# Experts 1 to 7 in float32 from whole-expert weight places, in an attention and two-FFN kernel

## The chip, the cores and the metric

The kernel runs on one core of a Trainium2 chip. The metric is the time of one execution on the device in microseconds: the median over runs, 895.2 us for the kernel before (three runs, 892.25 to 896.22). The profile is of one execution of its own.

## The reference, cut to what matters

Three steps follow one another. Block-causal attention over 4 batches, 8 heads, 576 positions and 64 columns gives 2304 tokens of 512 columns. A leaky FFN follows, whose weights are float64. The last step is a mixture of experts:

```python
do_compute = x @ w_skip > 0                    # the others pass through
logits = x @ w_gate;  e_idx = argmax(logits)   # one of 8 experts for a token
h = np.maximum(x[mask] @ w1[e], 0.0)           # 512 -> 1024
y[mask] = gate_w * (h @ w2[e])                 # 1024 -> 512
out = x + y
```

Each expert has 2 MB of w1 and 2 MB of w2 in float32. How many tokens an expert has is known only when the kernel runs.

## The kernel before, in words

Phase A is the attention with the first quarter of the FFN, phase B the rest of the FFN over six blocks of 384 tokens (`b_mm1`, `b_mm2`), each followed by its routing. What this document is about comes last, the experts.

**Precision.** Most products are made from three float32r matmuls: each operand is split into a high part, rounded to float32r, and a low part, the remainder, and high x high, high x low and low x high are summed in PSUM (`products`, L852). The attention's first four pairs of heads (`WHOLE`, L23) instead multiply in float32 at one point, the product with V (L285).

**One expert tile** (`expert_tile`, L885) takes 128 gathered tokens. `turn_x` (L844) transposes them on PE; ACT copies the high part, DVE subtracts the low part. `m1` has two halves of 12 matmuls of 512 columns; ACT applies relu (L897), PE transposes the hidden layer (`turn_h`, L902), ACT copies its high part (L903), DVE subtracts its low part (L904), and `m2` has 24 matmuls of 512 columns. `finish` scales the sum and adds the residual on DVE (L941) and scatters the rows to the output from POOL (L942). The matmuls are held in the program's order (`keep_in_program_order`); other instructions are put in order by a planner, which issues what is ready.

**The weights.** A piece is 128 rows of 512 columns. `load_piece` (L795) loads it from SP's queue to one of twelve places (tiles "raw", "cv2", "cv3"); `split_piece` (L815) casts it to its high part on ACT or DVE (L825), subtracts the low part on DVE or POOL (L826), and then issues the load that takes its place. An expert has 16 pieces, and each has its parts in one of two buffers (`w1buf`, `w2buf`), which lie in the FFN's weight tiles `wbt[0..5]` and in its input `xT`. While one expert multiplies, its tile's `fill` splits the next expert's 16 pieces, in portions (`SOME`, `SOME1`). Loads of expert 1 beyond the first six pieces are `held` back behind the loads of the lists, in program order (L1012).

**Which tiles run.** Expert 0 has up to four tiles and a loop, experts 1 to 7 one tile, then conditional ones. Each condition is a `tc.If` on the expert's count (L1043), so each engine takes a branch there; expert 7 as a whole stands in such a condition (L1030). The scatters show eleven tiles in this run: four of expert 0, one each of experts 1 to 6, and a second one of expert 2. Expert 7 has no tokens, and its pieces are split all the same, during expert 6. A tile's `ahead` transposes the tokens of the next tile before its own last matmuls.

**Order before the experts.** Expert 0's first tile runs beside the routing of the last block. Its second tile's tokens come by a gather that POOL issues behind that routing, then POOL writes the lists, and SP loads them back (`load_lists`, L599) once the first tile has ended; four more gathers follow.

Of the kernel before, what the change touches and what calls it, by code (L numbers as in the profile page):

```python
# [347 lines left out]
def attention_moe_kernel(  # L348
# [27 lines left out]
    NB = NT // BT  # L376
    HALF = NT // 2
    KS = 4

    SOME, SOME1 = (3, 4, 3, 6), (0, 2, 4, 10)  # L380

    C = ctx.enter_context(tc.tile_pool(name="c", bufs=1))
    DR = ctx.enter_context(tc.tile_pool(name="dr", bufs=1, space=DRAM))
# [392 lines left out]
    def lane(L, n, xg, xt):  # L776

        return dict(li=L["li"][:, n], ix=L["ix"][:, n], xg=xg, xh=xt[0], xl=xt[1],
                    xT=[(xt[0][:, c], xt[1][:, c]) for c in range(ND)])


    pair = lambda x, y: [[wbt[(x, y)[c // 2]][:, i, c % 2 * F2 : c % 2 * F2 + F2] for c in range(ND)] for i in range(2)]
    w1buf = [pair(wi_at[0], wi_at[1]), pair(wi_at[2], wo_at[2])]
    w2buf = [[[xT[i][:, f % ND, f // ND * D : (f // ND + 1) * D] for f in range(NF2)] for i in range(2)],
             [[wbt[wo_at[f // 4]][:, i, f % 4 * D : f % 4 * D + D] for f in range(NF2)] for i in range(2)]]


    tags = ("raw", None, "cv2", "cv3") * 3
# [1 line left out]

    begin = [NP - NF2 + f for f in range(ND)] + list(range(NP - NF2)) + [NP - NF2 + f for f in range(ND, NF2)]
    AHEAD = len(tags)
    raws, held = {}, []

    def load_piece(i):  # L795
        e, j = divmod(i, NP)
        j = j if e else begin[j]
        if e >= E:
            return
        nm = tags[i % AHEAD]  # L800
        n = 2 if nm == "raw" else 1
        t = CV.tile([128, n, 512], F32, name=nm, bufs=3)
        for k_ in range(n):
            raws[i + k_] = t[:, k_]
        if j < NP - NF2:
            h, c = divmod(j, ND)
            src = w1[e, c * 128 : (c + n) * 128, h * 512 : h * 512 + 512]
        else:
            f = j - (NP - NF2)
            src = w2[e, f * 128 : (f + n) * 128, :]  # L810
        ld = nc.sync.dma_start(t, src.rearrange("(n p) w -> p n w", p=128))
        if i in held:
            tc.keep_in_program_order(ld)

    def split_piece(i):  # L815
        e, j = divmod(i, NP)
        j = j if e else begin[j]
        a, b = w1buf[e % 2], w2buf[e % 2]
        if j < NP - NF2:
            h, c = divmod(j, ND)  # L820
            hi, lo = (a[k_][c][:, h * 512 : h * 512 + 512] for k_ in range(2))
        else:
            hi, lo = (b[k_][j - (NP - NF2)] for k_ in range(2))
        r = raws.pop(i)
        tc.keep_in_program_order(nc.vector.tensor_copy(hi, r) if i % 4 == 3 else nc.scalar.copy(hi, r))  # L825
        (nc.gpsimd if i % 3 == 2 else nc.vector).tensor_tensor(out=lo, in0=r, in1=hi.bitcast(F32), op=ALU.subtract)  # L826
        nm = tags[i % AHEAD]
        if nm == "raw":
            return
        nxt = i + AHEAD - (nm is None)  # L830
        if e == 0 and nxt >= NP + 6:
            held.append(nxt)
        else:
            load_piece(nxt)

    upto = [0]

    def w_steps(n):

        l = [lambda i=i: split_piece(i) for i in range(upto[0], min(n, E * NP))]  # L840
        upto[0] = max(n, upto[0])
        return l

    def turn_x(lx, pt=None, pinned=True):  # L844
        pin = tc.keep_in_program_order if pinned else lambda ins: ins
        pt = ps3.tile([128, ND, 128], F32, name="pt", tag="ps") if pt is None else pt
        for c in range(ND):
            pin(nc.tensor.transpose(pt[:, c], lx["xg"][:, c * 128 : (c + 1) * 128], ident))
        nc.scalar.copy(lx["xh"], pt)
        nc.vector.tensor_tensor(out=lx["xl"], in0=pt, in1=lx["xh"].bitcast(F32), op=ALU.subtract)  # L850

# [30 lines left out]
                    pt=lambda: bank("acc1", 4, 128),  # L882
                    yo=lambda: CV.tile([128, 512], F32, name="cv2", bufs=3))

    def expert_tile(e, lx, fill=(), ahead=(), late=False, at=None, between=None):  # L885

        a, b = w1buf[e % 2], w2buf[e % 2]
        at = at or places()
        hh, hl, ph, py = at["hh"], at["hl"], at["ph"], at["py"]
        fs = [slice(f * 512, f * 512 + 512) for f in range(2)]  # L890
        m1 = [products(ph[f], lx["xT"], [(a[0][c][:, fs[f]], a[1][c][:, fs[f]]) for c in range(ND)]) for f in range(2)]
        m2 = products(py, [(hh[:, c], hl[:, c]) for c in range(NF2)], [(b[0][c], b[1][c]) for c in range(NF2)])
        h = {}

        def relu(f):
            h[f] = at["hs"](f)
            nc.scalar.activation(out=h[f], in_=ph[f], func=AF.Relu)  # L897

        def turn_h(f):
# [6 lines left out]
        fill, share = list(fill), SOME1 if late else SOME  # L906

        def some(n):
            run_all(fill[:n])
            del fill[:n]  # L910

        some(share[0])
# [6 lines left out]
        some(share[1])  # L919
        relu(0)  # L920
        run_all(m1[1][:7])
        if between:
            between[2]()
        turn_h(0)
        some(share[2])
        run_all(m1[1][7:])
        relu(1)
        if not late:
            run_all(ahead)
        run_all(m2[:4])  # L930
        turn_h(1)
        some(share[3])
        run_all(m2[4:18])
        if late:
            run_all(ahead)
        run_all(m2[18:])
        some(len(fill))
# [8 lines left out]
        return finish  # L946

    seq = [(n, f) for a, b in cuts for n in order[:3] for f in range(a, b)]
    seq += [(n, f) for n in order[3:] for f in range(NFB)]
# [45 lines left out]
    finish = expert_tile(0, first, at=places_early(),  # L995
                         ahead=[lambda: turn_x(second, ps2.tile([128, ND, 128], F32, name="rtx", tag="acc0", bufs=1), True)], late=True,
                         between=(lambda: run_all(begin_r), lambda: run_all(route_r), place_and_put))
    end = finish()
    cnti = RC.tile([128, E], I32, name="cnti")
# [8 lines left out]
    with tc.issue_after(end.ins):  # L1008
        for k_ in (2, 1, 0, 3):
            load_lists(lall[k_], lambda l: l.rearrange("(e n) c -> n e c", e=E)[k_ * 128 : (k_ + 1) * 128], nc.sync)  # L1010
            find(lall[k_])
    for i in held:  # L1012
        load_piece(i)
    p2.close()
    ps3 = ctx.enter_context(tc.tile_pool(name="ps3", bufs=7, space=PSUM))
    M3 = ctx.enter_context(tc.tile_pool(name="m3", bufs=2))
# [4 lines left out]
    firsts = [lane(lall[0], e, xgs[e % 4], xts[e % 2]) for e in range(E)]  # L1021
    fourth = lane(lall[3], 0, xgs[0], xts[2])
    for lx in (firsts[1], fourth, firsts[2], firsts[3]):
        gather(lx)
    for e in range(E):
        ahead1 = [lambda: turn_x(firsts[e + 1])] if e + 1 < E else []
        some = ExitStack()
        if e:
            if e == E - 1:
                some.enter_context(tc.If(nreg[e] > 0))  # L1030
            second = lane(lall[1], e, xgs[4], xts[2])
            gather(second)
            finish = expert_tile(e, firsts[e], w_steps((e + 2) * NP), ahead1, at=places(True))

        def later(k_):
            if e == 0 and k_ == 3:
                return fourth
            L, n = (lall[k_], e) if k_ < KS else (llate, 0)
            return lane(L, n, xgs[4 + (k_ + 1) % 2], xts[2 + (k_ + 1) % 2])

        def more(k_, lx):
            filled = e == 0 and k_ == 1
            with nullcontext() if filled else tc.If(nreg[e] > 128 * k_):  # L1043
                if k_ == 1 and not filled:
                    turn_x(lx)
                if k_ < KS:
                    ahead = []
                    nx = later(k_ + 1)
                    if k_ + 1 < KS:
                        if nx is not fourth:  # L1050
                            gather(nx)
                        ahead = [lambda: turn_x(nx)]
                    finish = expert_tile(e, lx, w_steps(2 * NP) if filled else (), ahead + (ahead1 if filled else []), True)
                    finish()
                    more(k_ + 1, nx)
                else:
                    with tc.For_i(KS, (nreg[e] + 127) // 128, 1) as i:
                        load_lists(llate, lambda l: l[bass.ds(i * 128 + e * NT, 128), :].unsqueeze(1), nc.sync)
                        find(llate)
                        gather(lx)  # L1060
                        turn_x(lx)
                        expert_tile(e, lx)()

        more(1, second)
        if e:
            finish()
        if e + 4 < E:
            gather(firsts[e + 4])
        some.close()
# [31 lines left out]
```

## Time and profile before

| | |
|---|---|
| median of three runs | 895.2 us |
| profiled execution, its span | 892.16 us, 890.3 us |
| PE busy | 804.6 us, 90% |
| DVE, ACT, POOL busy | 532.4, 463.3, 401.9 us |
| mean granted clock of TensorE | 0.98 |
| moved by DMA | 110.64 MB, 124 GB/s over the span |

The span runs from the first to the last instruction. Matmuls are pipelined and overlap in the records, so a pace is read from start to start. "PEq", "DVEq" and the like are the engines' sequencers, which handle branches and waits. The last stretch, some 200 us, is the experts'.

### The profile page before, as it was taken

How to read it: one execution, taken by the hardware profiler on the slowest of the kernel's cores; microseconds unless marked ns; L12 is line 12 of the kernel's file. 1: busy time of each engine (PE TensorE's matmuls, PEld its weight loads, DVE VectorE, ACT ScalarE, POOL GpSimd, SP SyncE). 2: the span in 40 equal slices, each digit the busy share in tenths (PEclk: the TensorE clock that was granted, in tenths of full speed). 3: DMA queues.
4: the chain of work that ended last, by engine and by line, in shares of the span. 5: the costliest groups of instructions: out<-in, count | busy, mean ns of one | idle time of the engine just before them, and what ended most of it. 6: DMA issues, size and time to landing. Idle time of an engine off the chain costs nothing. (4 is left out here: it accounts for less than half of the span.)

```text
span 890.3 us, 13976 instructions
## 1 busy us (share of the span) xinstructions
PE 804.6 (90%) x4754; PEld 717.1 (81%) x4754; DVE 532.4 (60%) x1026; ACT 463.3 (52%) x1054; POOL 401.9 (45%) x472
## 2 busy tenths in 40 slices
PE   6789999999999988989999999999999869788683
PEld 4567899989989987879989898989899658566462
DVE  6887888878787896894132222121133671776897
ACT  5787779878787866662222222222234232534453
POOL 3766446455455664653324333222243350544463
PEclk9999999999999999999999999999999989999998
DMA  6664563563431255732204150302022691664772
GB/s 163 154 168 120 158 149 91 128 186 89 104 85 43 76 175 142 250 129 77 71 1 115 64 153 25 107 1 70 26 60 98 146 318 52 211 228 159 245 248 86
DMA packets 120596, 110.64 MB, mean 124 GB/s; under 512 B 77285, under 2 KB 87525, under 8 KB 120496
## 3 DMA queue, kind: packets, MB, share of 16 engines
q1 hardware_dynamic: 112320, 93.35, 36.3%
q0 software_dynamic: 8176, 16.06, 6.1%
q8 instruction: 51, 0.84, 0.4%
q14 instruction: 49, 0.40, 0.1%
HBM read 78.87 MB, written 22.68 MB: 114 GB/s over the span
## 5 line engine op out<-in xcount | busy, mean ns | idle before, releaser
L441 PE MATMUL ph<-xT,wbt 128*128 128x384 f32 x864 | 164.9, 339 | 4.3 <-ACT cv L488 2.5
L441 PE MATMUL acc<-gh,wbt 128*128 128x384 f32 x576 | 162.1, 341 | 3.6 <-DVE x2T L773 2.5
L441 PEld LDWEIGHTS ph<-xT,wbt 128*128 128x128 f32 x864 | 152.2, 189 | 4.9 <-ACT cv L488 2.7
L433 POOL TENSOR_TENSOR gl<-u,gh 128x384 fp32r<-128x384 f32 x72 | 74.6, 1036 | 177.4 <-ACT gh L432 177.3
L432 DVE TENSOR_TENSOR u<-ph,u 128x384 f32<-128x384 f32 x72 | 40.0, 555 | 179.3 <-ACT u L431 179.3
L441 PEld LDWEIGHTS acc<-gh,wbt 128*128 128x128 f32 x576 | 105.1, 188 | 11.3 <-issue 8.0
L185 POOL TENSOR_SCALAR P<-P,stat 128x128 f32<-128x128 f32 (+2 forms) x144 | 78.6, 567 | 58.2 <-DVE stat L183 43.9
L441 PE MATMUL acc<-gl,wbt 128*128 128x384 f32 x288 | 97.8, 340 | 0.6 <-POOL gl L433 0.6
L432 ACT CAST gh<-u 128x384 fp32r<-128x384 f32 x72 | 36.9, 512 | 93.2 <-PE acc L441 90.3
L431 ACT ACTIVATE u<-ph 128x384 f32<-128x384 f32 x72 | 35.3, 490 | 93.7 <-PE ph L441 88.2
L285 PE MATMUL pv<-ph,vs 128*128 128x320 f32 (+4 forms) x280 | 70.0, 319 | 2.1 <-DVE ph L239 0.8
L236 PE MATMUL pt<-ident,P 128*128 128x128 f32 x400 | 63.5, 286 | 3.8 <-ACT P L174 2.7
L161 PE MATMUL sp<-wbt 128*128 128x128 f32 (+2 forms) x192 | 55.5, 371 | 10.8 <-DMA wbt<-wbt 3.3
L441 PE MATMUL po<-gA,woa 128*128 128x320 f32 (+1 forms) x384 | 60.2, 302 | 3.4 <-DVE xf L300 1.4
L412 POOL TENSOR_TENSOR cv<-cv,cv 128x512 int32<-128x512 int32 x32 | 44.3, 1389 | 39.4 <-DVE cv L411 22.8
L441 PE MATMUL ph<-xT,wia 128*128 128x320 f32 (+1 forms) x384 | 58.9, 301 | 1.9 <-DVE cv L432 1.9
L243 DVE TENSOR_TENSOR pl<-pt,ph 128x512 fp32r<-128x512 f32 (+2 forms) x84 | 50.5, 627 | 16.9 <-ACT ph L242 15.6
L441 PEld LDWEIGHTS po<-gA,woa 128*128 128x128 f32 x384 | 53.0, 189 | 6.5 <-DVE xf L300 2.0
L285 PEld LDWEIGHTS pv<-ph,vs 128*128 128x128 f32 x280 | 50.6, 189 | 7.8 <-DVE cv L432 1.7
L441 PEld LDWEIGHTS acc<-gl,wbt 128*128 128x128 f32 x288 | 54.3, 189 | 2.9 <-issue 1.9
L441 PEld LDWEIGHTS ph<-xT,wia 128*128 128x128 f32 x384 | 53.0, 189 | 3.2 <-DVE cv L432 2.5
L236 PEld LDWEIGHTS pt<-ident,P 128*128 128x128 f32 x400 | 47.9, 146 | 7.7 <-ACT P L174 3.2
(232 smaller groups left out, 1735.5 us busy)
## 6 DMA issues: line engine op xcount, KB each, us to landing
raw<-in_moe_w_dram SPq DMA_DIRECT2D x32, 512.0 KB, 5.0
cv<-in_moe_w_dram SPq DMA_DIRECT2D x64, 256.0 KB, 4.7
wbt<-wbt SPq DMA_DIRECT2D x60, 144.0 KB, 2.5
raw<-in_moe_w_in_dram SPq DMA_DIRECT2D x16, 512.0 KB, 4.2
raw<-in_moe_w_out_dram SPq DMA_DIRECT2D x16, 512.0 KB, 4.3
xTd<-xT POOLq DMA_DIRECT2D x4, 1152.0 KB, 8.2
x2T<-part_d SPq DMA_DIRECT2D x6, 768.0 KB, 5.5
xT<-xTd POOLq DMA_DIRECT2D x6, 768.0 KB, 6.4
```

The source lines that it names most:

```text
L161: nc.tensor.matmul(o_, st()[a][h][:, rows : rows + m], st()[b][:, h, c : c + w], start=(i == 0), stop=(i == 1))
L185: nc.gpsimd.tensor_scalar(out=P, in0=P, scalar1=rs[:, i : i + 1], scalar2=1.0, op0=ALU.mult, op1=ALU.mult)
L236: nc.tensor.transpose(o, src, self.ident)
L243: nc.vector.tensor_tensor(out=dl, in0=s_, in1=dh.bitcast(F32), op=ALU.subtract)
L285: nc.tensor.matmul(box["pv"][:, c0:N], v, box[t][:, i, h, cs], start=(jc == 0 and t == "ph"), stop=(jc == runs[-1][0] and t == parts[-1]))
L412: nc.gpsimd.tensor_tensor(out=w, in0=w, in1=low, op=ALU.add)
L431: nc.scalar.activation(out=u, in_=ph, func=AF.Copy, scale=0.01)
L432: return [nc.vector.tensor_tensor(out=u, in0=ph, in1=u, op=ALU.max), nc.scalar.copy(gh, u), nc.gpsimd.tensor_tensor(out=gl, in0=u, in1=gh. ...
L433: nc.gpsimd.tensor_tensor(out=gl, in0=u, in1=gh.bitcast(F32), op=ALU.subtract)]
L441: nc.tensor.matmul(ps, x, y, start=first and m == 0, stop=last and m == 3 * n - 1)
```

## The change: what it does

Expert 0 stays as it was. Experts 1 to 7 are no longer split. `load_expert` loads a whole expert in eight transfers of 512 KB from SP's queue, to one of four places used in turn: `wbt[1]` with `wbt[4]`, `wbt[3]` with `wbt[5]`, `wbt[0]` with `wbt[2]`, and the two `xT` tiles. Experts 1 and 2 are loaded, in the code, after the lists; these loads aren't held in program order. Experts 3 and 4 follow after expert 0's tiles, and expert e + 4 after expert e's.

`expert_tile32` multiplies in float32: four matmuls of 512 columns for each half of the hidden layer and eight for the output, 16 in place of 48. The tokens and the hidden layer have one part: `turn_x` copies half on ACT and half on DVE, `turn_h` makes one DVE copy. `expert_tile` loses its `fill`, so that expert 0's second tile no longer splits expert 1.

```diff
+    def load_expert(e):
+        if e >= E:
+            return
+        k_ = (e - 1) % 4
+        if k_ < 3:
+            x, y = ((wo_at[0], wo_at[1]), (wi_at[2], wo_at[2]), (wi_at[0], wi_at[1]))[k_]
+            a, b = ((WA if t < 2 else WB).tile([128, 2, 4 * 512], F32, name=f"wbt{t}").rearrange("p i w -> p (i w)") for t in (x, y))
...
+        else:
+            a, b = (C.tile([128, ND, HALF], F32, name=f"xT{i}") for i in range(2))
...
+        for c in range(ND):
+            nc.sync.dma_start(a[:, c], w1[e, c * 128 : (c + 1) * 128])
+        for c in range(ND):
+            nc.sync.dma_start(b[:, c], w2[e, c * 256 : (c + 1) * 256].rearrange("(k p) w -> p k w", p=128))
...
     def load_piece(i):
-        e, j = divmod(i, NP)
-        j = j if e else begin[j]
-        if e >= E:
+        if i >= NP:
             return
+        j = begin[i]
...
+        if "xw" in lx:
+            nc.scalar.copy(lx["xw"][:, 0:2], pt[:, 0:2])
+            nc.vector.tensor_copy(lx["xw"][:, 2:4], pt[:, 2:4])
+            return
...
+    def expert_tile32(e, hw, lx, ahead=(), at=None):
...
+        def turn_h(f):
+            pt = at["pt"]()
+            for c in range(4):
+                tc.keep_in_program_order(nc.tensor.transpose(pt[:, c], h[f][:, c * 128 : (c + 1) * 128], ident))
+            nc.vector.tensor_copy(hw[:, 4 * f : 4 * f + 4], pt)
+
+        for c in range(ND):
+            mm1(0, c)
+        relu(0)
+        for c in range(2):
+            mm1(1, c)
+        turn_h(0)
+        for c in range(2, ND):
+            mm1(1, c)
+        relu(1)
+        for f in range(2):
+            mm2(f)
+        turn_h(1)
+        for f in range(2, 6):
+            mm2(f)
+        run_all(ahead)
+        for f in range(6, NF2):
+            mm2(f)
+        return finisher(lx, at, py)
...
-    for i in held:
-        load_piece(i)
+    for e in (1, 2):
+        load_expert(e)
...
         if e:
             finish()
+            load_expert(e + 4)
+        else:
+            load_expert(3)
+            load_expert(4)
```

## Rows read from the trace of the kernel before

**Rows 1.** Windows: length, busy us (count) of PE, PEld, DVE, ACT, POOL; clock, DMA, GB/s.

```profile
60.00:66.00 6.00, 6.00 (x34) 4.86 (x33) 5.17 (x11) 4.00 (x11) 1.78 (x2) 1.00 0.67 214
...
695.00:700.00 5.00, 4.26 (x29) 3.42 (x29) 4.15 (x23) 1.64 (x4) 0.00 (x0) 1.00 0.97 363
...
730.00:735.00 5.00, 4.34 (x10) 3.47 (x11) 3.49 (x7) 0.00 (x0) 2.17 (x2) 0.50 1.02 362
...
740.00:760.00 20.00, 19.46 (x91) 15.46 (x90) 5.63 (x9) 6.07 (x11) 2.02 (x2) 1.00 0.04 15
...
820.00:840.00 20.00, 14.95 (x60) 11.02 (x60) 17.05 (x20) 9.50 (x18) 10.95 (x9) 0.91 0.72 231
```

**Rows 2.** Waits, 684 to 891 us: who waited for whom, us, times, longest.

```profile
PE ph L856 <- PEq L1043: 10.3, 5, 3.9
...
PE py L856 <- DVE hl L904: 10.0, 8, 2.6
```

**Rows 3.** PE in order of time, expert 0's last three tiles: start, us, instructions [idle].

```profile
723.00 0.66 PE L848 MATMUL pt<-ident,xg 128*128 128x128 f32 x4 [1.01 <-DMA xg<-x_d,la0ix]
...
727.66 0.73 PE L856 MATMUL ph<-wbt,xt 128*128 128x512 f32 x2 [2.60 <-ACT xt L849]
730.66 6.42 PE L856 MATMUL ph<-wbt,xt 128*128 128x512 f32 x17 [2.27 <-DVE xt L850]
...
745.06 4.57 PE L856 MATMUL ph<-wbt,xtf 128*128 128x512 f32 x19
749.47 0.60 PE L902 MATMUL pt<-ident,hs 128*128 128x128 f32 x4
749.82 1.42 PE L856 MATMUL ph<-wbt,xtf 128*128 128x512 f32 x5
...
757.88 4.66 PE L856 MATMUL ph<-wbt,xt 128*128 128x512 f32 x19 [0.54 <-PEq L1043]
```

**Rows 4.** ACT in order of time, between expert 0's second and third tiles.

```profile
725.47 0.62 ACT L825 CAST wbt<-cv 128x512 fp32r<-128x512 f32 x1 [3.60 <-DMA cv<-in_moe_w_dram]
...
727.03 1.06 ACT L849 CAST xt<-pt 128x512 fp32r<-128x512 f32 x2
```

**Rows 5.** PE in order of time, float32 matmuls in the attention.

```profile
62.15 3.45 PE L285 MATMUL pv<-ph,vs 128*128 128x320 f32 x12
65.44 0.60 PE L236 MATMUL pt<-ident,P 128*128 128x128 f32 x4
```

**Rows 6.** Branches of PE's sequencer at L1043: least/median/most ns, first and last start.

```profile
L1043 PEldq COMPARE_BRANCH  x1: 187/187/187, 757.5 to 757.5; - x1
...
L1043 PEldq COMPARE_BRANCH  x1: 5000/5000/5000, 769.6 to 769.6; - x1
```

**Rows 7.** PE in order of time, start of expert 2 and end of expert 6.

```profile
774.90 2.56 PE L856 MATMUL ph<-wbt,xtf 128*128 128x512 f32 x10 [2.78 <-PEq L1043]
...
877.45 0.39 PE L856 MATMUL py<-xT,hl 128*128 128x512 f32 x1
```

**Rows 8.** POOL in order of time, behind the last scatter.

```profile
881.79 1.29 POOL L826 TENSOR_TENSOR wbt<-raw,wbt 128x512 fp32r<-128x512 f32 x1
```

**Rows 9.** PE in order of time, phase B's last matmul.

```profile
687.40 0.34 PE L441 MATMUL acc<-gh,wbt 128*128 128x384 f32 x1
```

**Rows 10.** SP in order of time, loads and stores issued around 324 to 351 us.

```profile
324.69 1.31 SPq L584 DMA_DIRECT2D list<-raw  x3
...
350.95 0.34 SPq L489 DMA_DIRECT2D part_d<-cv  x1
```

**Rows 11.** Gathers: POOL's issue, first use on PE, and landings, early and late.

```profile
701.33 0.97 POOL L605 DMA_INDIRECT xgf<-x_d,lfix  x1 [6.49 <-DVE cnti L1000]
...
L848 PE MATMUL rtx<-ident,xgf x4: 272/272/273, 707.5 to 707.8; 128*128 128x128 f32 x4
...
DMA to landing us min/median/max: 3.3/3.3/3.3
...
DMA to landing us min/median/max: 5.4/7.2/7.3
```

More of the change, by code (lines that the diff above doesn't have):

```diff
@@ L378, in attention_moe_kernel @@
     KS = 4
-    SOME, SOME1 = (3, 4, 3, 6), (0, 2, 4, 10)
     C = ctx.enter_context(tc.tile_pool(name="c", bufs=1))
@@ L779, in lane, with lane32 @@
                     xT=[(xt[0][:, c], xt[1][:, c]) for c in range(ND)])
[L782 to L785, printed above, removed]
+    def lane32(L, n, xg, xt):
+        return dict(li=L["li"][:, n], ix=L["ix"][:, n], xg=xg, xw=xt)
+    w1buf = [[wbt[wi_at[c // 2]][:, i, c % 2 * F2 : c % 2 * F2 + F2] for c in range(ND)] for i in range(2)]
+    w2buf = [[xT[i][:, f % ND, f // ND * D : (f // ND + 1) * D] for f in range(NF2)] for i in range(2)]
+    weights = {}
+    def load_expert(e):
[5 more added lines that the diff above has]
+            a, b = ((WA if t < 2 else WB).tile([128, 2, 4 * 512], F32, name=f"wbt{t}").rearrange("p i w -> p (i w)") for t in (x, y))
+            a, b = a.rearrange("p (c w) -> p c w", w=F2), b.rearrange("p (c k w) -> p c k w", k=2, w=D)
+        else:
+            a, b = (C.tile([128, ND, HALF], F32, name=f"xT{i}") for i in range(2))
+            a, b = a[:, :, 0:F2], b[:, :, 0 : 2 * D].rearrange("p c (k w) -> p c k w", k=2)
+        for c in range(ND):
+            nc.sync.dma_start(a[:, c], w1[e, c * 128 : (c + 1) * 128])
+        for c in range(ND):
+            nc.sync.dma_start(b[:, c], w2[e, c * 256 : (c + 1) * 256].rearrange("(k p) w -> p k w", p=128))
+        weights[e] = [a[:, c] for c in range(ND)], [b[:, f // 2, f % 2] for f in range(NF2)]
     tags = ("raw", None, "cv2", "cv3") * 3
@@ L792, in attention_moe_kernel @@
     AHEAD = len(tags)
-    raws, held = {}, []
+    raws = {}
     def load_piece(i):
-        e, j = divmod(i, NP)
-        j = j if e else begin[j]
-        if e >= E:
+        if i >= NP:
             return
+        j = begin[i]
         nm = tags[i % AHEAD]
@@ L806, in load_piece @@
             h, c = divmod(j, ND)
-            src = w1[e, c * 128 : (c + n) * 128, h * 512 : h * 512 + 512]
+            src = w1[0, c * 128 : (c + n) * 128, h * 512 : h * 512 + 512]
         else:
             f = j - (NP - NF2)
[L810 to L813, printed above, removed]
+            src = w2[0, f * 128 : (f + n) * 128, :]
+        nc.sync.dma_start(t, src.rearrange("(n p) w -> p n w", p=128))
     def split_piece(i):
-        e, j = divmod(i, NP)
-        j = j if e else begin[j]
-        a, b = w1buf[e % 2], w2buf[e % 2]
+        j = begin[i]
         if j < NP - NF2:
             h, c = divmod(j, ND)
-            hi, lo = (a[k_][c][:, h * 512 : h * 512 + 512] for k_ in range(2))
+            hi, lo = (w1buf[k_][c][:, h * 512 : h * 512 + 512] for k_ in range(2))
         else:
-            hi, lo = (b[k_][j - (NP - NF2)] for k_ in range(2))
+            hi, lo = (w2buf[k_][j - (NP - NF2)] for k_ in range(2))
         r = raws.pop(i)
@@ L827, in split_piece @@
         nm = tags[i % AHEAD]
[L828 to L834, printed above, removed]
+        if nm != "raw":
+            load_piece(i + AHEAD - (nm is None))
     upto = [0]
     def w_steps(n):
-        l = [lambda i=i: split_piece(i) for i in range(upto[0], min(n, E * NP))]
+        l = [lambda i=i: split_piece(i) for i in range(upto[0], n)]
         upto[0] = max(n, upto[0])
@@ L883, in places_early, with expert_tile @@
                     yo=lambda: CV.tile([128, 512], F32, name="cv2", bufs=3))
-    def expert_tile(e, lx, fill=(), ahead=(), late=False, at=None, between=None):
-        a, b = w1buf[e % 2], w2buf[e % 2]
+    def expert_tile(lx, ahead=(), at=None, between=None):
+        a, b = w1buf, w2buf
         at = at or places()
@@ L904, in turn_h @@
             nc.vector.tensor_tensor(out=hl[:, 4 * f : 4 * f + 4], in0=pt, in1=hh[:, 4 * f : 4 * f + 4].bitcast(F32), op=ALU.subtract)
[L906 to L912, printed above, removed]
         run_all(m1[0][:6])
@@ L918, in expert_tile @@
             between[1]()
-        some(share[1])
         relu(0)
@@ L924, in expert_tile, with finisher @@
         turn_h(0)
-        some(share[2])
         run_all(m1[1][7:])
         relu(1)
-        if not late:
-            run_all(ahead)
         run_all(m2[:4])
         turn_h(1)
-        some(share[3])
         run_all(m2[4:18])
-        if late:
-            run_all(ahead)
+        run_all(ahead)
         run_all(m2[18:])
-        some(len(fill))
+        return finisher(lx, at, py)
+    def finisher(lx, at, py):
         def finish():
@@ L946, in expert_tile, with mm1, mm2, relu @@
         return finish
+    def expert_tile32(e, hw, lx, ahead=(), at=None):
+        a, b = weights[e]
+        at = at or places()
+        ph, py = at["ph"], at["py"]
+        h = {}
+        def mm1(f, c):
+            tc.keep_in_program_order(nc.tensor.matmul(ph[f], lx["xw"][:, c], a[c][:, f * 512 : f * 512 + 512], start=(c == 0), stop=(c == ND - 1)))
+        def mm2(f):
+            tc.keep_in_program_order(nc.tensor.matmul(py, hw[:, f], b[f], start=(f == 0), stop=(f == NF2 - 1)))
+        def relu(f):
+            h[f] = at["hs"](f)
+            nc.scalar.activation(out=h[f], in_=ph[f], func=AF.Relu)
+        def turn_h(f):
[17 more added lines that the diff above has]
+            mm2(f)
+        run_all(ahead)
+        for f in range(6, NF2):
+            mm2(f)
+        return finisher(lx, at, py)
     seq = [(n, f) for a, b in cuts for n in order[:3] for f in range(a, b)]
@@ L993, in place_and_put @@
             run_all(put_r)
-    finish = expert_tile(0, first, at=places_early(),
-                         ahead=[lambda: turn_x(second, ps2.tile([128, ND, 128], F32, name="rtx", tag="acc0", bufs=1), True)], late=True,
+    finish = expert_tile(first, at=places_early(),
+                         ahead=[lambda: turn_x(second, ps2.tile([128, ND, 128], F32, name="rtx", tag="acc0", bufs=1), True)],
                          between=(lambda: run_all(begin_r), lambda: run_all(route_r), place_and_put))
@@ L1020, in attention_moe_kernel @@
     xts = [xtf[0], xts[0], xtf[1], xts[1]]
-    firsts = [lane(lall[0], e, xgs[e % 4], xts[e % 2]) for e in range(E)]
     fourth = lane(lall[3], 0, xgs[0], xts[2])
+    xws = [CV.tile([128, ND, 128], F32, name=nm, bufs=3) for nm in ("cv2", "cv2", "cv3", "cv3")]
+    hw = [CV.tile([128, NF2, 128], F32, name="raw", bufs=3) for _ in range(2)]
+    firsts = [lane32(lall[0], e, xgs[e % 4], xws[e % 2]) for e in range(E)]
     for lx in (firsts[1], fourth, firsts[2], firsts[3]):
@@ L1030, in attention_moe_kernel @@
                 some.enter_context(tc.If(nreg[e] > 0))
-            second = lane(lall[1], e, xgs[4], xts[2])
+            second = lane32(lall[1], e, xgs[4], xws[2])
             gather(second)
-            finish = expert_tile(e, firsts[e], w_steps((e + 2) * NP), ahead1, at=places(True))
+            finish = expert_tile32(e, hw[0], firsts[e], ahead1, at=places(True))
         def later(k_):
@@ L1038, in later @@
             L, n = (lall[k_], e) if k_ < KS else (llate, 0)
-            return lane(L, n, xgs[4 + (k_ + 1) % 2], xts[2 + (k_ + 1) % 2])
+            return (lane32 if e else lane)(L, n, xgs[4 + (k_ + 1) % 2], (xws if e else xts)[2 + (k_ + 1) % 2])
+        tile_of = (lambda *a: expert_tile32(e, hw[1], *a)) if e else expert_tile
         def more(k_, lx):
@@ L1052, in more @@
                         ahead = [lambda: turn_x(nx)]
-                    finish = expert_tile(e, lx, w_steps(2 * NP) if filled else (), ahead + (ahead1 if filled else []), True)
+                    finish = tile_of(lx, ahead + (ahead1 if filled else []))
                     finish()
@@ L1061, in more @@
                         turn_x(lx)
-                        expert_tile(e, lx)()
+                        tile_of(lx)()
         more(1, second)
```

## The prediction

> **What bounds the kernel now.** I read the windows first, then the waits by total, then TensorE's order of time through the experts. The windows [rows 1] show two things. From 740 to 760 us, where expert 0's last two tiles run and nothing is loaded, PE is busy 19.46 of 20 us; from 820 to 840, among experts 3 and 4, it is busy 14.95, while DVE is busy 17.05, ACT 9.50 and POOL 10.95 and the DMA engines 72%. So the experts' stage is TensorE's when nothing is being split, and is shared with the splitting when something is. The waits [rows 2] name the places: PE stood 10.3 us in five waits at the branch of L1043, the longest 3.9, and 10.0 us in eight waits for DVE's low half of the hidden layer (L904). What ends a tile late is thus a small DVE or ACT instruction queued behind splits, and behind the splits a load (by the code a place for a piece comes free only when the piece in it has been split).
>
> The order of time on PE [rows 3] gives two anchors. Expert 0's fourth tile, in which no piece is split, runs from 745.06 to 757.34 (757.88 - 0.54): 12.28 us, with 19 float32r matmuls in 4.41 us, 0.232 us each, and four transposes in 0.35 us. Its second tile ends at 725.06 (727.66 - 2.60), and the third can't go on until 730.66: PE waits 2.60 us for ACT's copy of x and 2.27 us for DVE's. ACT's rows [rows 4] say why: that copy started at 727.03 behind a split that had itself waited 3.60 us for a weight transfer.
>
> **The change part by part.**
>
> *Removed: 7 x 16 splits.* From the code, each piece is one cast and one subtraction. They lie on DVE, ACT and POOL, so in themselves they are worth nothing; what counts is the waits above.
>
> (a) Expert 0's second to fourth tiles lose the filling. The second ends about where it did, less the wait of 1.01 us for a gather at 723.00 [rows 3]: 724.1. The third then starts at once and takes the fourth's 12.28 plus four transposes of x, 0.35: 736.7. The fourth ends at 749.0 instead of 757.34. That is 8.3 us; I take 8.0. Lower bound: the two idle times alone, 4.9. Upper: 8.9, if the first part of the second tile gains too.
>
> (b) *Added: float32 matmuls.* Each tile of experts 1 to 6 has 16 matmuls of 512 columns instead of 48. The trace has float32 matmuls in the first four pairs of the attention (L285). By the count (56 in the code, 112 records more than the split ones) each is two records with a weight load apiece, and twelve records of 320 columns start at 62.15 and give way at 65.44 [rows 5]: 0.274 us each at full granted clock (60 to 66 us in rows 1). By columns, 512 make 0.439 us; 32 records are 14.04 us. [...] From above: twice the pace of the float32r matmul of 512 columns, 0.464, 14.85 us. I take 0.439, the row nearest in kind. With eight transposes of h and four of x (12 x 0.0875) a tile is 15.1 us of PE. Nothing else should stand inside it: ACT's relu has two matmuls, 1.75 us, before its transposes, and the one DVE copy, without a low half behind it, has 1.75 us again; copies of that size took ACT 0.53 us each (two in 1.06, rows 4).
>
> (c) *The branch.* After each expert PE's sequencer takes a branch over three unused tiles and a loop. It took 5.00 us at 769.6, after expert 1, against 0.19 at 757.5, after expert 0 [rows 6]. Of the 5.00 PE stood 2.78 [rows 7]: the rest, some 2.2 us, is the ten matmuls (10 x 0.232) queued since the last wait of the tile. In the new tile the last wait is for the copy of the second half of h, some 1.3 us after its transposes (an estimate, two and a half such copies); behind it lie the rest of six float32 matmuls and a transposition, 6 x 0.877 + 0.35 - 1.3 = 4.3 us. A branch of 5 us then shows 0.7, one that made PE stand 3.9 shows 1.8 (3.9 + 2.2 - 4.3), a short one little: 4 us over five of them, another 1.0 before expert 2's second tile (its x is turned on the spot) and 0.5 before expert 1. Bounds: 2 and 11.3 (before's 10.3 at the branches and the 1.0).
>
> The stage of seven tiles lasted from 757.88 to 877.84 [rows 3, 7], 119.96 us. Now 7 x 15.1 + 5.0 = 110.7. Gain 9.3, from -3 (gaps as before, 0.464 us a record) to 14 (gaps of 2 us, 0.427).
>
> [...]
>
> (d) *The tail.* After the last matmul, DVE scales, POOL scatters, and then POOL still splits a piece of expert 7, which has no tokens: 1.29 us at 881.79 [rows 8]. That goes: 1.3, from 0 (something else ends as late) to 2.2.
>
> (e) *Moved: the loads.* 28 MB in 16 x 512 KB per two experts, now waiting for a place and not for splits. The places of experts 1 and 2 come free one after the other while the first FFN's last block runs, the last of them when its last matmul, at 687.40, is done [rows 9]; the code gives that their loads stand behind the lists, but they are not held in program order. The planner moves such loads ahead: L584 stands after the whole first phase in the code, yet was issued at 324.69, before L489 at 350.95 [rows 10]. So I expect 8.4 MB to move from well before 687 to about 700, at up to 363 GB/s (695 to 700 in rows 1). What they are moved past on SP: the last block's three stores to x_d and the twelve list loads. What profits: from 714 on nothing is loaded, so the gathers should land in 3.3 us, as the early ones did, rather than 7.2 [rows 11], which removes the 1.01 us in (a). The second gather, issued at 701.33 and landing 3.3 us later, is first used at 707.5 [rows 11]: 2.9 us of slack. I cost the move at nothing; the rival has its price if that cover goes. Experts 3 and 4 load from 749: 8.4 MB at that rate take 23 us, until 772, and are needed at about 797 and 813; later ones have as much room. Issuing 16 loads at 0.44 us (three in 1.31 in rows 10) takes SP 7 us, done before the next branch at 764.
>
> [...]
>
> **Sum.** 8.0 + 9.3 + 1.3 = 18.6 us. From the profiled run (892.16, span 890.3) that makes 873.6; the median of the runs is 895.2, 3.0 above it. Forecast for the median: 876.
>
> **Rivals.**
> *Small transfers.* The early loads hold up the stores to x_d, the second gather and the lists. For: they are hoisted, and gathers took 7.2 us under load. Against: the places come free one after the other, so the queue is at most 4 MB deep. Price: 4.2 MB at 363 GB/s, 11.6 us, less the 2.9 of slack: 8.7; time 885.
> *Gaps stay.* The branch still costs before's 10 us and a record takes 0.45 us: (b, c) give next to nothing; time 885. [...] Against: the PE work queued ahead of it doubles.
> [...]
> [...]
>
> **How the numbers follow.** The forecast's own case, 870 to 880, has 0.56. Short branches 0.10, small transfers 0.14, gaps stay 0.12, clock 0.08. Range 864 to 889: it takes in the rivals on the fast side and the two at 885, and leaves out the clock and the ends of two bounds together. A difference under 0.5% (4.5 us) can't be told from none here. Faster: 0.56 + 0.10 + 0.12 + 0.08 = 0.86. Same 0.06, from "small transfers" (0.02) and "gaps stay" (0.04) at their worst; slower 0.08, the clock.
>
> **What would show it.** (a) Third tile of expert 0 starting within 1 us of the second's end, expert 1 at about 749. (b) Records of L285's kind at 0.43 to 0.46 us in the experts, granted clock 1.0 from 750 on. (c) PE's waits at the branch under 6 us in all; none for DVE's copy of h. (d) No DVE cast after the last scatter. (e) Loads of experts 1 and 2 before 700 us, an idle DMA from 714 to 749. Wrong it would be if PE waits for a weight transfer in any expert, if the second tile starts after 712, or if a float32 tile takes over 17 us.

## The result, and the profile after

The changed kernel takes 881.8 us (median of four runs, 879.99 to 883.51) against 895.7 for the kernel before in the same comparison: ratio 0.9852, interval 0.9819 to 0.9885. It is faster, by 13.9 us; the forecast was 876 us, the range 864 to 889.

The profiled execution took 879.99 us, its span is 878.2, 12.1 less than before. The windows that answer to [rows 1] (same columns):

```profile
695.00:700.00 5.00, 5.00 (x25) 2.92 (x24) 4.97 (x7) 2.03 (x4) 2.33 (x2) 0.91 0.66 242
730.00:735.00 5.00, 5.00 (x26) 3.93 (x25) 0.69 (x1) 1.78 (x3) 0.97 (x1) 1.00 0.33 107
740.00:760.00 20.00, 19.46 (x78) 13.05 (x77) 3.89 (x6) 2.96 (x5) 3.01 (x3) 1.00 0.33 125
820.00:840.00 20.00, 18.34 (x53) 8.68 (x52) 2.56 (x4) 1.57 (x3) 4.44 (x5) 1.00 0.75 266
```

Among experts 3 and 4, DVE's busy time falls from 17.05 to 2.56 us while PE's rises from 14.95 to 18.34: the stage is now TensorE's, but for one wait of 1.66 us that comes up below. The half clock of 730 to 735 (0.50) is gone (1.00). The waits that answer to [rows 2]:

```profile
PE ph L958 <- PEq L1091: 4.3, 4, 1.8
...
PE py L870 <- DVE hl L918: 1.4, 1, 1.4
```

PE in order of time (start, us, instructions, idle ahead) gives where the time went; it answers to [rows 3, 7, 9]:

```profile
688.12 0.34 PE L439 MATMUL acc<-gh,wbt 128*128 128x384 f32 x1
688.31 0.60 PE L858 MATMUL py<-ident,xgf 128*128 128x128 f32 x4
...
712.96 4.67 PE L870 MATMUL ph<-wbt,xtf 128*128 128x512 f32 x19
...
727.64 4.59 PE L870 MATMUL ph<-wbt,xt 128*128 128x512 f32 x19
...
740.20 4.57 PE L870 MATMUL ph<-wbt,xtf 128*128 128x512 f32 x19
...
753.03 5.39 PE L958 MATMUL ph<-wbt,cv 128*128 128x512 f32 x12 [0.54 <-PEq L1091]
...
770.10 5.39 PE L958 MATMUL ph<-wbt,cv 128*128 128x512 f32 x12 [1.77 <-PEq L1091]
...
836.36 5.31 PE L958 MATMUL ph<-wbt,cv 128*128 128x512 f32 x12 [1.66 <-DVE yo L943]
...
865.38 1.88 PE L961 MATMUL py<-wbt,raw 128*128 128x512 f32 x4
```

Read from anchor to anchor, the 12.1 us are these. Up to the issue of expert 0's first gather (677.81 us before, 678.95 after) 1.1 are lost, in stages that the change doesn't touch: the 1.1 are there before the first early load is issued, and in the thirteen profiles of this document the gather is issued anywhere from 677.1 to 684.2. From there to the second tile's start 2.3 are lost: 31.70 us before, 34.01 now. From the second tile to expert 1, 8.3 are gained: 40.07 for 48.37. The experts' stage, 753.03 to 867.26, takes 114.2 for 119.96: 5.7 gained. The tail gains 1.5 (10.9 for 12.5).

The loss of 2.3 us is the one that the prediction had at nothing. The transposes of expert 0's first tokens stood 22 matmuls ahead of phase B's end before, at 683.32; now they stand behind its last matmul. ACT's splits of expert 0's weights are queued behind the copy that follows them, as ACT's order of time shows:

```profile
688.94 0.58 ACT L863 CAST xtf<-py 128x512 fp32r<-128x512 f32 x1 [4.09 <-PE py L858]
689.42 1.14 ACT L840 CAST wbt<-raw 128x512 fp32r<-128x512 f32 x2
```

These splits began at 684.43 before. On DVE the routing stands behind the last of the splits, and PE waits for the routing's result (`ohb`). The last split and that wait, before and after:

```profile
695.76 0.69 DVE L826 TENSOR_TENSOR xT<-cv,xT 128x512 fp32r<-128x512 f32 x1
697.67 0.17 PE L658 MATMUL lt<-ohb,U 128*128 128x8 bf16 x1 [0.34 <-DVE ohb L653]
...
699.82 0.69 DVE L841 TENSOR_TENSOR xT<-cv,xT 128x512 fp32r<-128x512 f32 x1
701.74 0.17 PE L656 MATMUL lt<-ohb,U 128*128 128x8 bf16 x1 [1.31 <-DVE ohb L651]
```

Counted from the gather's issue, the last split and PE's go-ahead come 2.9 us later (22.79 for 19.86); from there to the second tile it is 11.2 us for 11.8, which leaves the 2.3. SP's issues (answering to [rows 10] in kind) show what had been put ahead:

```profile
658.05 0.80 SPq L802 DMA_DIRECT2D wbt<-in_moe_w_dram  x2
...
676.01 3.78 SPq L804 DMA_DIRECT2D wbt<-in_moe_w_dram  x4
...
688.50 1.92 SPq L804 DMA_DIRECT2D wbt<-in_moe_w_dram  x4
```

The branches (least/median/most ns, first and last start), answering to [rows 6], after experts 1, 2, 3 and 4:

```profile
L1091 PEldq COMPARE_BRANCH  x1: 6200/6200/6200, 763.6 to 763.6; - x1
...
L1091 PEldq COMPARE_BRANCH  x1: 3449/3449/3449, 796.9 to 796.9; - x1
...
L1091 PEldq COMPARE_BRANCH  x1: 5997/5997/5997, 813.1 to 813.1; - x1
...
L1091 PEldq COMPARE_BRANCH  x1: 343/343/343, 830.0 to 830.0; - x1
```

### The profile page after: what moved, and what is told of

Its sections match the earlier page's. It is cut to its first block, busy times and chain, and to the rows that moved or that the text cites. A ratio compares the mean times of both kernels' runs of the same rounds, so it can differ in the third digit from the quotient of the medians.

```text
span 878.2 us, 13305 instructions
## 1 busy us (share of the span) xinstructions
PE 815.6 (93%) x4642; PEld 693.9 (79%) x4642; DVE 437.3 (50%) x923; ACT 409.2 (47%) x956; POOL 347.3 (40%) x435
```

## The experiments

Two questions were open. Is it the early loads that cost expert 0's first tile its 2.3 us, and by which way? And what makes a branch take 0.3 or 6 us, which decides the gaps? A third measure was the price of float32 against that of the splits.

The first tile has an anchor that the variation of earlier stages doesn't touch, the time from the issue of its tokens' gather to the start of the second tile. All runs by it, with PE's wait in the routing for DVE's `ohb` (L651; L653 in the kernel before) and the granted clock behind that wait, by windows of 5 us:

| kernel | transposes | gather to second tile, us | wait for `ohb`, us | clock behind it |
|---|---|---|---|---|
| before; before_short | early | 31.70; 31.68 | 0.34; 0.34 | 1.00 |
| turned2; best; best_again | early | 32.23; 32.14; 32.36 | 1.36; 1.37; 1.38 | 1.00 |
| pinned; nosplit | early | 33.88; 33.88 | 1.92; 1.92 | 0.50; 0.63 |
| after; short; ks3; noload | late | 34.01; 33.98; 34.02; 34.01 | 1.31; 2.98; 2.98; 1.32 | 1.00 |
| after_again; short_again | late | 36.82; 36.69 | 2.98; 2.98 | 0.63; 0.50 |

### after_again: the changed kernel once more

> The changed kernel once more, as the measure for the three beside it. Both theories: 0.985 of the kernel before. Theory 'order of issue': the transposes of expert 0's first tokens stand behind phase B's last matmul in the program itself, so again 24 to 25 us from phase B's last matmul to the first matmul of expert 0's second tile (21.9 in the kernel before). Rival 'chance': the first profile's 24.7 us was one execution's; now 22 to 23.

880.5 us, ratio 0.9847 (0.9822 to 0.9872). The transposes stand again behind phase B's last matmul (686.48 behind 686.30), and it is 27.6 us to the second tile, more than either theory said: behind PE's wait of 2.98 us the clock fell, and 700 to 705 was granted 0.63. The order is the program's and repeats; that fall of the clock doesn't come in each execution.

### pinned: the loads of experts 1 and 2 held behind the lists

```diff
-            nc.sync.dma_start(a[:, c], w1[e, c * 128 : (c + 1) * 128])
+            ld = nc.sync.dma_start(a[:, c], w1[e, c * 128 : (c + 1) * 128])
+            if pin:
+                tc.keep_in_program_order(ld)
...
-        load_expert(e)
+        load_expert(e, True)
```

The loads of w2 are held in the same way.

> The loads of experts 1 and 2 are held in program order behind the loads of the lists. Theory 'order of issue' (the planner puts the transposes of expert 0's first tokens behind all of phase B because it counts the early loads as traffic in front of the gather): without them the transposes stand 22 matmuls earlier, as before; 21.9 to 22.5 us from phase B's last matmul to the second tile; 2 to 2.7 us faster than the changed kernel, less up to 1.5 us given back where the second gather and the lists now land beside the loads: 878.5 to 880.5 us where the changed kernel has 881.8. Rival 'chance': no difference here, and the loads at 710 to 750 us delay the gathers: 882 to 884.

882.2 us, ratio 0.9853 (0.983 to 0.9877): no difference from the changed kernel, as the rival had it, but not for its reason. The order did come back, the time didn't. PE's order of time and the window:

```profile
683.71 0.60 PE L862 MATMUL py<-ident,xgf 128*128 128x128 f32 x4
...
698.10 0.17 PE L656 MATMUL lt<-ohb,U 128*128 128x8 bf16 x1 [1.92 <-DVE ohb L651]
...
698.33 2.37 PE L874 MATMUL eph<-wbt,xtf 128*128 128x512 f32 x7
```

```profile
700.00:705.00 5.00, 5.00 (x18) 4.31 (x17) 1.41 (x6) 0.59 (x1) 2.00 (x2) 0.50 0.13 34
```

PE came to this wait 17.96 us behind the gather's issue (19.52 before), and DVE let it go on at 19.88, as before (19.86). From there to the second tile it is 14.0 us for 11.8: the matmuls behind the wait ran at a granted clock of 0.50, seven took 2.37 us, 1.87 before. Also PE waited 1.16 us for the third tile's tokens, beside the loads (1.01 before). So the first half of the theory is shown (the early loads are what moves the transposes), the second, that this returns 2 us, is not: a fall of the clock took it back.

### turned2: loads early, transposes put back

```diff
-            turn_x(first, psx.tile([128, ND, 128], F32, name="py", bufs=1), False)
+            turned = turn_x(first, psx.tile([128, ND, 128], F32, name="py", bufs=1), False)
...
-            add = b_mm2(n, f)
+            with tc.issue_after(turned.ins) if i >= len(seq) + lag - 2 else nullcontext():
+                add = b_mm2(n, f)
```

`turned` is `turn_x`'s last transposition of expert 0's tokens.

> The loads stay early; only the last two steps of phase B's second multiplication (24 matmuls) are put behind the transposes of expert 0's first tokens on PE. Theory 'order of issue': the order alone costs the 2.7 us, so it returns: 879 to 879.8 where the changed kernel has 881.8. Rival 'the gather lands late' (the early loads hold up the gather's data, the planner was right): PE waits 2 to 4 us for the gathered tokens ahead of the transposes, with phase B's last matmuls queued behind: 881.5 to 884.

878.6 us, ratio 0.9811 (0.9788 to 0.9834), 1.9 us under the changed kernel beside it; the two intervals overlap a little. By the trace both theories have a share:

```profile
685.60 0.63 PE L858 MATMUL py<-ident,xgf 128*128 128x128 f32 x4 [1.22 <-DMA xgf<-x_d,lfix]
```

The gather, issued at 679.02, is ready only 6.6 us later, where before it had landed 3.3 us after its issue and was used 5.5 us after it without a wait; PE stands 1.22 us for it. The planner had a reason to put the transposes later, and put them too late: the second tile still starts 1.8 us sooner (table).

### short: two tiles less for a branch to skip

```diff
+        ks = 2 if e else KS
...
-                if k_ < KS:
+                if k_ < ks:
...
-                    with tc.For_i(KS, (nreg[e] + 127) // 128, 1) as i:
+                    with tc.For_i(ks, (nreg[e] + 127) // 128, 1) as i:
```

Left for a branch to skip are the second tile and the loop with its one tile.

> Experts 1 to 7 keep the first and the second conditional tile and the loop; the third and fourth conditional tile are left out of the program (they would be run by the loop), so that a branch skips half as much code. Theory 'distance': the long branches (6.2 and 6.0 us after experts 1 and 3) become 0.2 to 3.5 us and the gaps in the experts' stage fall from 7.4 to 3 to 5 us: 878 to 880. Rival 'the branch waits on the DMA engines or on a fetch of any distance': branches as now, 881 to 882.5.

874.0 us, ratio 0.9767 (0.9745 to 0.9788): 6.5 us under the changed kernel beside it, more than the theory said. The branches after experts 1, 2 and 3, and expert 2's start on PE:

```profile
L1093 PEldq COMPARE_BRANCH  x1: 332/332/332, 766.9 to 766.9; - x1
...
L1093 PEldq COMPARE_BRANCH  x1: 212/212/212, 798.7 to 798.7; - x1
...
L1093 PEldq COMPARE_BRANCH  x1: 220/220/220, 814.3 to 814.3; - x1
```

```profile
771.95 5.39 PE L958 MATMUL ph<-wbt,cv 128*128 128x512 f32 x12 [0.30 <-PEq L1093]
```

The stage, 756.36 to 866.08, takes 109.7 us, 4.5 less: 4.1 from the idle times (7.35 to 3.2, of it 1.25 ahead of expert 5) and 0.44 from four transposes for a third tile that the second no longer makes. The tail is 2.7 shorter (8.2 for 10.9). PE's branch over expert 7, which skips less code too, took 0.41 us for 3.36, but that isn't what ends the kernel: in `ks3`, below, it took 3.83 us and the tail is 8.2 as well. What is gone in both is a pause of POOL between its last scatter and its closing instructions (0.2 to 0.4 us from one to the other, 2.98 in the changed kernel); its cause isn't shown. That the loads kept the DMA engines at a share of 1.0 from 760 to 792 in this run and no branch was long rules out traffic alone.

### noload: no weight transfers behind 700 us

```diff
+        if e >= 3:
+            weights[e] = weights[2 - e % 2]
+            return
```

> The changed kernel without the loads of experts 3 to 7, which multiply the weights of experts 1 and 2 instead (time only). No weight transfer is under way behind 700 us; the code that a branch skips is the same. Theory 'the fetch goes through the DMA engines': branches that took 6.2 and 6.0 us with the engines full take 3.3 to 3.7, as they did with the engines idle in the kernel before without splits; their gaps, 1.8 and 1.6 us, go to 0.3 to 0.5, and 2 to 3 us are saved: 877.5 to 879 where the changed kernel has 881. Which branches are long stays as it is. Rival 'distance alone': 6 us as now, 881. Rival 'traffic alone': all branches 0.3 us, 876 to 877.

878.7 us, ratio 0.9809 (0.9781 to 0.9837); the interval overlaps the changed kernel's, so the trace has to decide. After experts 1 and 3:

```profile
L1094 PEldq COMPARE_BRANCH  x1: 3493/3493/3493, 762.1 to 762.1; - x1
...
L1094 PEldq COMPARE_BRANCH  x1: 3315/3315/3315, 810.2 to 810.2; - x1
```

```profile
767.14 5.39 PE L961 MATMUL ph<-wbt,cv 128*128 128x512 f32 x12 [0.30 <-PEq L1094]
```

As the theory had it: the same branches are long (the third, after expert 2, took 3.60), each at 3.3 to 3.6 us, and what PE has queued covers that (it is busy 3.50 of the 3.50 us of the first), so that the gap is 0.30 for 1.77. Idle times are 3.2 us in all.

### ks3: one tile less

The edit of `short` with 3 for 2.

> The changed kernel with only the fourth conditional tile of experts 1 to 7 left out: a branch skips three tiles' code on PE, between the four of the changed kernel (long after experts 1, 2, 3, short after 4, 5, 6) and the two with which all were short. Theory 'the target is at hand or it is not, by where the code falls': fewer long branches than three of six, each 3.3 to 6.3 us and none between 0.5 and 3: 875 to 880. Rival 'in proportion': each long branch three quarters as long, 4.6 us, and still three of them: 879 to 880.

877.1 us, ratio 0.9779 (0.9748 to 0.9809). Two branches were long, after experts 3 and 5, where the second was short in the changed kernel:

```profile
L1093 PEldq COMPARE_BRANCH  x1: 4606/4606/4606, 818.5 to 818.5; - x1
...
L1093 PEldq COMPARE_BRANCH  x1: 3815/3815/3815, 849.7 to 849.7; - x1
```

```profile
823.55 5.39 PE L958 MATMUL ph<-xT,cv 128*128 128x512 f32 x12 [0.30 <-PEq L1093]
```

So long or short was not in proportion to the code skipped; it went by place (after experts 3 and 5 here, after 1 to 3 in the changed kernel). And 4.6 us was no more than the queue covered: 0.30 is what a short branch leaves too.

### before_short: the edit of `short` in the kernel before

> The kernel before, splits and all, with the third and fourth conditional tile of experts 1 to 7 left out of the program. A branch then skips two tiles of 60 matmuls and transposes each on PE, about as many instructions as the changed kernel's branch skips (four tiles of 28), where the changed kernel's branches took 6.2, 3.4, 6.0 and three times 0.3 us. Theory 'distance in instructions': a mix of long and short branches here too, PE's waits at the branches fall from 10.3 to 4 to 7 us: 888 to 892. Rival 'number of tiles or conditions': all branches short, as with two tiles in the changed kernel: 884 to 887. Rival 'the long branch is a matter of DMA traffic': no change, 895.

890.8 us, ratio 0.9944 (0.992 to 0.9968): 5.3 us. One branch in the experts was long and one took 0.96, and PE's waits at the branches fell from 10.3 us to 3.7 (expected 4 to 7). The profiled execution is the slowest of the ten (895.86 us), late by 6.4 us before the experts begin; in its experts' stage those 6.6 us gave only 1.5 (118.5 for 119.96), and the waits (whom PE waited for, us, times, longest) show where the rest went:

```profile
L1045 PEldq COMPARE_BRANCH  x1: 5546/5546/5546, 823.7 to 823.7; - x1
```

```profile
PE py L856 <- DVE hl L904: 15.0, 7, 4.3
...
PE ph L856 <- PEq L1045: 3.7, 5, 2.0
```

The wait for DVE's half of the hidden layer rose from 10.0 to 15.0. That fits a tile that starts sooner and meets splits that are no further on; no run tests it. As the theory by distance had it, the mix of long and short is back at this amount of code, though with fewer long ones than in the changed kernel.

### nosplit: the kernel before without loads and splits of experts 1 to 7

```diff
-        if e >= E:
+        if e >= 1:                            # load_piece
             return
...
+        if e:                                 # split_piece
+            return
```

> The kernel before with neither loads nor splits of experts 1 to 7: those experts multiply stale split weights, 48 float32r matmuls a tile, so that only the time is read. What the waits for splits and loads cost in all, and from it the price of float32. Theory: a tile then takes what expert 0's fourth tile takes with four more transposes, 12.6 us, and the gaps at the branches stay at 10 to 11 us: seven tiles 99 us where the kernel before has 119.96 and the changed kernel 114.2; with 8 us from expert 0 and 1.3 at the end about 865. So float32 would cost 2.7 us a tile, 19 in all, and the splits' waits 21 plus the 8 of expert 0. Rival 'the waits are not the splits' (the half-size matmuls of the hidden layer still wait for DVE's subtraction): 13.5 us a tile, 872.

863.7 us, ratio 0.9642 (0.9609 to 0.9675), 1.3 under the forecast of 865. First and last matmul of the stage, and a branch with its window:

```profile
754.03 4.66 PE L858 MATMUL ph<-wbt,xt 128*128 128x512 f32 x19 [0.54 <-PEq L1045]
...
850.42 0.40 PE L858 MATMUL py<-xT,hl 128*128 128x512 f32 x1
```

```profile
L1045 PEldq COMPARE_BRANCH  x1: 3300/3300/3300, 763.5 to 763.5; - x1
```

```profile
763.50:766.80 3.30, 3.27 (x14) 2.28 (x13) 0.00 (x0) 0.00 (x0) 0.00 (x0) 1.00 0.02 7
```

The stage takes 96.8 us, 6.3 of it idle, so 12.9 a tile. The kernel before lost 23.2 us of the stage (119.96 less 96.8) to loading and splitting; float32 costs 2.4 us a tile (15.3 for 12.9), 17 in all. The change bought the one with the other. The six long branches took 3.3 to 3.7 us with nothing loading (3.4 to 6.0 before), with the code that they skip unchanged, and PE's waits there fell from 10.3 to 2.8. The 1.3 us expected at the end didn't come: the tail is 12.3 us for 12.5.

### best and best_again: short branches and the transposes put back

Both edits, with `short` once more beside them.

> The kernel with the third and fourth conditional tile left out of experts 1 to 7, once more, as the measure for the next one. 0.977 of the kernel before; all branches of the experts under 0.5 us.

> Both edits that were faster: short branches, and phase B's last 24 matmuls behind the transposes of expert 0's first tokens. Theory 'independent costs': the order is worth as much as by itself, 1.5 to 2.5 us off the kernel with short branches alone: 871.5 to 872.5. Rival 'the order's gain was a lucky clock' (the second tile's start hangs on where the granted clock falls, not on the order): no difference, 873.5 to 875.

> Both faster edits once more, as a second measure: 0.975 of the kernel before (0.974 to 0.976); PE's wait for DVE's routing in expert 0's first tile under 1.5 us and no stretch under full granted clock behind it. If the order is worth nothing: 0.9765 to 0.978, as the kernel with short branches alone in its first measure.

`short` 873.8 us, ratio 0.9755 (0.9728 to 0.9782); both edits 872.0, 0.975 (0.9723 to 0.9778), and again 873.7, 0.9764 (0.9735 to 0.9792). These are the fastest versions that do all the work, 22 to 24 us under the kernel before and about 8 under the changed one, but the times don't tell the two edits from `short` alone, and the second measure lies just between the ranges of its two theories. By the traces the second tile starts 1.7 us sooner with the order put back than where `short` and `ks3` kept their clock, and 4.4 sooner than where it fell. In `best_again` the second tile itself then lost 1.9 us (42.2 to expert 1 for 40.3): PE waited 2.01 us for DVE, and 720 to 725 was granted 0.66. How many executions have such a fall isn't known, so what the order is worth on the mean stays open between 0 and about 2 us.

## Why the prediction was right, and where it was wrong

The direction, the bound and the main mechanism held: PE was kept waiting by splits, and without them it pays float32 and still gains (`nosplit`: 23.2 us lost to loads and splits, 17 paid for float32). By the steps:

(a) Predicted 8.0, measured 8.3. The third tile starts without a wait at 727.64, the fourth at 740.20; from the second's start it is as written. That gain lies behind a later start, below.

(b) The pace was right: twelve records, two a matmul, from 753.03 to 758.26 make 0.436 us each, predicted 0.439 from twelve records of 320 columns. The granted clock was 1.0 from 700 to 860, so the slower clock that had 0.08 did not come; that float32 matmuls bring the clock down no run shows. The tiles sum to 107.4 us instead of 105.7: between these float32 records four transposes take 0.43 us, not the 0.35 taken from among float32r matmuls, and expert 2's first tile has four more of them. Mis-sized by 1.7.

(c) Behind expert 1's start the idle times are 6.8 us against 5.0 for all gaps. At the branches it is 4.7 against 4, before expert 2's second tile 0.46 against 1.0; so the rival "gaps stay" fell. The formula held where it can be seen: 6.2 us of branch less 4.3 queued leaves 1.9, measured 1.77; 6.0 leaves 1.7, measured 1.57. (The 0.95 us behind expert 2's second tile hardly depends on the branch: it is 0.69 in `short`, where the branch took 0.21.) Its inputs did not: taken as 5 us with the engines loaded, the branch took 6, and three of six were short, which made up for it. That the branches' sum came out near is luck; "short branches" (0.10), all of them short like the 0.19 us at 757.5, was true of three of the six: 0.31 to 0.34 us, while the other three took 3.4 to 6.2. Nearly all of the excess is a wait of 1.66 us ahead of expert 5, which no term had. The profile puts it down to DVE's scaling, but that had ended at 835.49. It comes again in `after_again`, `pinned` and `turned2` (1.55, 1.70, 1.31); `short` and `ks3`, with less code, and `noload`, with the same code for PE and no loads, have 0.30 to 0.41. So it takes this code and the loads together; the cause isn't shown.

Two readings of the working were off, and nothing hangs on either. The 0.19 us at 757.5 is the second of two records behind expert 0; such a second one comes only behind experts 0 and 2, in which conditional tiles ran. The branch over unused code behind expert 0 is the one at 754.1, 0.36 us. And gaps of 2 us with records of 0.427 make a gain of 15, not 14; no run shows that 0.427 as a bound: in the changed kernel the records made 0.430 (eight from 779.63 to 783.07) to 0.436 us.

(d) Predicted 1.3, measured 1.5, but not by the way foretold: that is luck. DVE's scaling and POOL's scatter behind the last matmul, before and after, with POOL's first closing instruction:

```profile
878.53 0.68 DVE L826 TENSOR_TENSOR wbt<-cv,wbt 128x512 fp32r<-128x512 f32 x1
879.55 0.75 DVE L941 SCALAR_TENSOR_TENSOR yo<-py,la0li,xg 128x512 f32<-128x512 f32 x1 [0.34 <-DVEq L1043]
880.58 1.21 POOL L942 DMA_INDIRECT out_dram<-yo,la0ix  x1 [2.86 <-DVE yo L941]
L1069 POOLq INC_SWDGE_SEM  x1: 1298/1298/1298, 883.4 to 883.4; - x1
...
867.30 0.75 DVE L943 SCALAR_TENSOR_TENSOR yo<-py,la0li,xg 128x512 f32<-128x512 f32 x1 [0.89 <-PE py L961]
868.33 1.00 POOL L944 DMA_INDIRECT out_dram<-yo,la0ix  x1 [14.09 <-DVE yo L943]
L1121 POOLq INC_SWDGE_SEM  x1: 1298/1298/1298, 871.3 to 871.3; - x1
```

POOL's split went, but from the scatter to the closing instruction it is 2.98 us for 2.82: in place of the split stands a pause. What was gained lies ahead of the scatter, which starts 1.07 us behind the last matmul's end for 2.74, because DVE's scaling no longer stands behind subtractions for expert 7.

(e) This step failed: "I cost the move at nothing." The loads were issued where expected, from 658 us on, and no transfer of weights was late. But the second tile started at 712.96, later than the 712 named as a sign of error: 2.3 us were lost between the first gather's issue and there. `pinned` and `turned2` show the way: with the early loads in its program, the planner put a first transposition behind 22 matmuls, and ACT's splits behind it; with the transposition back, 1.8 of the 2.3 us return, and PE waits 1.2 us for the gather itself. The rival "small transfers" had the right place and the wrong way and price: no tile waited for lists, the one transfer that was held up is the first gather, and it was 2.3 us instead of 8.7. Nor were the DMA engines idle from 714 to 749: no weights moved, but from 720 to 725 their share was 0.58, with lists and gathers.

The sum: forecast 18.6, less 1.7 (tiles), 1.8 (gaps), 2.3 (first tile) and 1.1 (stages ahead), with 0.3 and 0.2 more from (a) and (d), is 12.2; the span fell by 12.1.

## What to carry to other kernels

When an edit lets a planner move transfers ahead, price what the planner will move in answer on every engine's queue in that stretch, not only the transfers. Work queued on PE ahead of a branch hid a long one up to about its own length (4.3 us by the prediction's estimate: a branch of 4.6 us left 0.30 us of idle time, one of 6.2 left 1.77). Leaving out copies of the seldom-run code that a branch skips brought the idle times of the stage in `short` from 7.35 to 3.2 us. A start made sooner didn't pay where the engine that it hands over to wasn't ready: in `pinned` it became a longer wait (1.92 us for 1.31) and a slower clock (0.50 for 1.00).

## What the runs showed of the hardware

A branch over unused code had one of two lengths in these profiles, about 0.2 to 0.4 us or 3.3 us and more (one of 0.96 lies between), and which it was went by its place in the program, not by traffic. In `short` no branch in the experts was long, with the engines full (a share of 1.0 from 760 to 792); in `noload` the same three were long as in the changed kernel, with the engines idle (0.02). The long ones were longer with traffic. Behind experts 1 to 6, in `before`, `before_short`, `nosplit`, `after`, `noload` and `ks3`, they took 3.3 to 3.8 us with the DMA engines' share at 0.02 to 0.04 (thirteen branches), 4.2 to 6.0 at 0.49 to 0.97 (seven), and 6.2 with the engines full (1.04, one). In the middle group the length doesn't follow the share (4.8 us at 0.84, 6.0 at 0.69). PE's branch over expert 7 took 3.4 us in the changed kernel and 4.6 in `before`, at a share of 0.10 in both, so traffic isn't all.

```profile
763.60:769.80 6.20, 4.72 (x14) 1.93 (x13) 1.18 (x2) 0.37 (x1) 0.00 (x0) 1.00 1.04 406
796.90:800.30 3.40, 3.40 (x12) 1.68 (x11) 0.00 (x0) 0.37 (x1) 0.00 (x0) 1.00 0.02 5
```

These are the windows of two long branches of the changed kernel; the last two columns are the DMA share and GB/s. The count of packets on one of the two queues named "instruction" (q8) goes with the number of long branches among these four: 48 in the changed kernel and in `noload`, 46 in `ks3`, 43 in `short`. Whether a long branch waits for such packets, and what makes it long at one place and short at another, isn't shown.

In expert 0's first tile the granted clock fell behind PE's wait for `ohb` in four of six executions with a wait of 1.92 or 2.98 us, and in none of seven with a wait of 0.34 to 1.38. In `after` and `noload` it had fallen earlier, from 690 to 695 us (0.74 and 0.66), behind three short waits of 1.67 us together that the other four with late transposes had too, with the clock at 1.00; PE then came later to the wait for `ohb`, and the second tile started at the same point. What decides whether the clock falls behind such a wait isn't shown.
